# An attention block on one core: the second shifted line of a chain by a transfer in place, without fills on GpSimd

## The chip, the cores and the metric

The kernel runs on one core of a Trainium2 chip. The core's engines are TensorE (matmuls; PE in the profile, its weight loads PEld), VectorE (DVE), ScalarE (ACT), GpSimd (POOL) and SyncE (SP), which only issues transfers here. The metric is the device time of one execution in microseconds, the median of several runs.

## The reference

`x` is 1 x 2048 x 448, `wqkv` 448 x 1344, `wo` 448 x 448, all in bfloat16; 16 heads of 28 channels.

```python
qkv = (x @ wqkv).reshape(B, S, 3, H, Dh).transpose(2, 0, 3, 1, 4)
q, k, v = qkv[0], qkv[1], qkv[2]
scores = einsum("bhqd,bhkd->bhqk", q, k) * Dh ** -0.5
p = softmax(scores, axis=-1)
o = einsum("bhqk,bhkd->bhqd", p, v)
return o.transpose(0, 2, 1, 3).reshape(B, S, D) @ wo
```

## The kernel before

**Tiles and sets.** The 16 heads are four groups (G) of four heads, each head padded to 32 partitions (HP). The 2048 queries are four chunks (c) of 512. A *set* is one group and one chunk, 16 sets in all, worked through in the list `ORDER`. In a set there are 4 heads x 16 blocks of 128 keys = 64 *halves*: one half is the 128 x 512 scores of one head, one block of keys and one chunk of queries. TensorE computes a half from K and Q (`emit_s`, line 780) into PSUM, one of two engines turns it into exponentials in bfloat16 in SBUF, and TensorE multiplies these with V and adds them into the set's output bank `o` (`do_pv`, line 1123). Four such products, one per head, run side by side in the array; they are called a wave. The row of ones that stands beside V in each head's 32 columns makes the softmax's sum come out with the output.

**Two ways to the exponential.** ScalarE takes two halves at once, from a pair of banks `a0` or `a1`, with its exponential function (`do_exp`, line 978), into one of 10 tiles `pt`. VectorE takes single halves from banks `d0`, `d1` and now and then `m`, without an exponential function: it adds a bias, clamps at zero and writes int16 (`do_a`, line 993, tile I). The integer, read as a bfloat16, is 2 to the power of the score with a straight line between powers of two. To smooth this, three such *lines* are summed: I itself, I + 43 and I + 85, as integers, each read as bfloat16 and multiplied with its own copy of V (`WT` = 1, 201/256, 159/256; the scaled copies are made on VectorE, `vs_job`, line 616). So a half on VectorE costs TensorE three products with V, and one on ScalarE a single one.

**Chains.** Four halves of VectorE, one for each head, stand side by side in one I tile of 128 x 2048: a chain. When it is full, the two additions are made for all four at once: line 1 into a tile J1, line 2 into a tile J2 (`do_add`, line 1064; `adds` is the queue of additions due, its third entry the next line to make). Some chains are *far*: when the chain opens with at least `FAR` = 30 halves of its set left, in sets 1 to 14, GpSimd fills the J1 tile with the constant 43 (`far_chain`, line 1029), and when I is full a transfer issued by GpSimd adds I into J1 (`accumulate`, line 1040, `accum_op=ALU.add`). VectorE then makes only line 2. There are 4 I tiles (`NCH`), 4 of J1 (`NJ`) and 3 of J2 (`NCH2`). A chain's tiles are free again when the products with V have used them.

**What sets the order.** The order of all engines' instructions is written out at build time by a planner (`plan`), which plays the program through with fixed costs: 0.904 us for an exponential of ScalarE, 0.6 for an eviction or a full addition on VectorE, 0.226 for a wave, 1.05 for a fill and 0.88 for the issue of an adding transfer on GpSimd, 5.6 from the end of the issue to its landing (`ACC_LAND`). It plays 24 random seeds and keeps the shortest. At each step the engine that is free first picks its next work (`pick_pe`, `pick_act`, `pick_dve`, `pick_pool`, `pick_sp`). VectorE gets a new half whenever a bank `d` is free, so the split between the two engines falls out of how fast VectorE empties its banks. Operations marked `port` on GpSimd and VectorE's additions are never placed at the same time (`port[...]`), and on the chip GpSimd's operations wait for the last such operation of VectorE that the planner placed ahead of them (`after_shared`). Chains open ahead of their set: when fewer than 20 halves of a set are left, VectorE's next chain is of the next set. The products with V, however, go set by set: the bank `o` opens for the next set only when every product of the last one has been made (`finish_set`).

**Other work on the same engines.** The projections of K, Q and V for the later groups run between (`k_job`, `q_job`, `v_job`); GpSimd squares K and Q for a bound on the scores (`square`, line 357) and multiplies finished outputs with the reciprocal of the sums (`mul`, line 1173); GpSimd also clears the tiles of V in the prologue (`clear_v`, line 241). V lies in one tile for each group (groups 2 and 3 together) and block of 512 keys, and so does each of the two scaled copies.

The lines that decide on a far chain:

```python
if sum(len(q) for q in remain[step[0]]) >= (FAR if step[0] < NSET - 1 else LASTFAR) and step[0] >= FIRST:
    ch["far"] = True
    far_chain(ch)
```

Of the kernel before, what the change touches and what calls it, by code (L numbers as in the profile page):

```python
# [9 lines left out]
ALU = mybir.AluOpType  # L10
# [43 lines left out]
def kernel(  # L54
# [36 lines left out]
    NPT = 10  # L91
    NCH = 4
    NCH2 = 3
    NJ = 4
    FAR = 30
    FIRST = 1
# [38 lines left out]
    WO = big.tile([P, G, D], BF16, name="WO")  # L135
    VT = [None] * NTERM
    for k in range(NTERM):
        VT[k] = {}
        for b in range(NXB):
            for g in range(GH):  # L140
                VT[k][g, b] = big.tile([P, XB, P], BF16, name=f"V{k}_{g}_{b}")[:]
        for b in range(NXB):
            t = big.tile([P, XB, G - GH, P], BF16, name=f"V{k}_{GH}_{b}")
            for g in range(GH, G):
                VT[k][g, b] = t[:, :, g - GH, :]
            VT[k][None, b] = t[:]
    xs = [big.tile([P, XB * D if b < NPL else (G - 1) * QW], BF16, name=f"xs{b}") for b in range(NXB)]
# [90 lines left out]
    def clear_v(g, b):  # L238
        v = VT[0][g, b]
        v = v.rearrange("p t g e -> p (t g e)") if g is None else v.rearrange("p t e -> p (t e)")  # L240
        nc.gpsimd.memset(v, 0.0)
        nc.gpsimd.memset(v.rearrange("p (r e) -> p r e", e=HP)[:, :, Dh:Dh + 1], 1.0)

    for g in list(range(GH)) + [None]:
# [13 lines left out]
    def plan(nc, tc, psum, big, wk, dram, seed, dry):  # L258
# [262 lines left out]
        def qn_first(bank, pri):  # L521
            def mm():
                held["qn0"] = (bank_tile(bank) if bank[0] != "a" else pair_tile(bank))[:, 0:QW]
                nc.tensor.matmul(out=held["qn0"], lhsT=maskK[:, 0, :], rhs=sqt.pop(("Q", 0, 0))[:], start=True, stop=True)

            def root():
                held["nq"] = VT[1][None, 0].rearrange("p t g e -> p (t g e)").bitcast(F32)
# [50 lines left out]
        def v_job(g, b, t0, bank, pri, gate=0, eng="DVE"):  # L578
# [7 lines left out]
            def mm(part):  # L586
                if part == 0:
                    held[key] = bank_tile(bank)
                for u in range(part * n // parts, (part + 1) * n // parts):
                    for cc in range(CC):  # L590
                        quarters(held[key][:, u * w:(u + 1) * w], xt(b, cc)[:, (t0 + u) * P:(t0 + u + 1) * P],
                                 WRAW[2][:, cc, g0 * HG * Dh:g1 * HG * Dh], cc == 0, cc == CC - 1)

            def evac():
                src = held.pop(key)[:, 0:n * w].rearrange("p (r e) -> p r e", e=Dh)
                if g is None:
                    dst = VT[0][None, b][:, t0:t0 + n, :, :].rearrange("p t g (i e) -> p (t g i) e", e=HP)
                else:
                    dst = VT[0][g, b].rearrange("p t (i e) -> p (t i) e", e=HP)
                if eng == "ACT":  # L600
                    nc.scalar.copy(out=dst[:, :, 0:Dh], in_=src)
                else:
                    nc.vector.tensor_copy(out=dst[:, :, 0:Dh], in_=src)

# [7 lines left out]

        def vs_job(g, b, pri):
            def scale(k):
                flat = (lambda v: v.rearrange("p t g e -> p (t g e)")) if g is None else (lambda v: v.rearrange("p t e -> p (t e)"))
                cur["shared"] = nc.vector.tensor_scalar(out=flat(VT[k][g, b]), in0=flat(VT[0][g, b]), scalar1=WT[k], scalar2=None, op0=ALU.mult)

            gs = [g] if g is not None else list(range(GH, G))
            for k in range(1, NTERM):
                add("DVE", 0.335 if g is None else 0.2, lambda k=k: scale(k), need=[("V", gs[0], XB * b + u) for u in range(XB)],  # L620
                    gives=[("VS", gg, b, k) for gg in gs], pri=pri + 0.1 * k, port=True)

# [110 lines left out]
        for b in range(NXB):  # L733
            v_job(1, b, 0, "m", 50 + b, STEPS + 10 + 12 * b)
            vs_job(1, b, 60 + b)
        a, z = 2 * STEPS, 2 * NQC * STEPS - 30
        for kt in range(0, NKT, 2):
            v_job(None, kt // XB, kt % XB, "m", 150 + kt, a + (z - a) * kt // NKT)
        for b in range(NXB):
            vs_job(None, b, 170 + b)  # L740
        for c in range(CL):
# [8 lines left out]
        pts_used = [0]  # L750
        chain = {"cur": None, "all": []}
        a_fifo = []
# [107 lines left out]
        def d_more(s, t, acting):  # L860
            got, taken = [], []
            for b in d_banks(t):
# [8 lines left out]
                if ch is None:  # L871
# [133 lines left out]
        def close(ch, m):  # L1005
            ch["m"] = m
            ch["at"] = free["DVE"]
            adds.append([ch, m, 2 if ch["far"] else 1])
            if ch["far"]:
                accumulate(ch, m)  # L1010

        def used_up(ch, k):
# [5 lines left out]
        def add_ok(a):  # L1018
            if a[2] == 1:
                return True  # L1020
            n = chain["all"].index(a[0])
            return n < NCH2 or used_up(chain["all"][n - NCH2], 2)

        def far_chain(ch):
# [8 lines left out]
            add("POOL", 1.05, emit, gives=[("fill", n)], pri=20, port=True)  # L1033

        def accumulate(ch, m):
            w = slice(0, m * QW)
# [5 lines left out]
            def landed(end):  # L1042
                at = ch["acc"] = end + ACC_LAND
                for n in range(m):
# [13 lines left out]
        def do_add(t):  # L1058
# [10 lines left out]
            adds[0][2] += 1  # L1069
            if adds[0][2] == NTERM:  # L1070
                adds.pop(0)
# [8 lines left out]
        def pv_cands(t):  # L1080
# [27 lines left out]
        def do_pv(t, ws):  # L1108
# [9 lines left out]
            for w in ws:  # L1118
                for e in w:
                    _, i, j = e["step"]  # L1120
                    key = (s, i)
                    SETMM[key] = SETMM.get(key, 0) + 1
                    nc.tensor.matmul(out=o[HP * i:HP * (i + 1), :], lhsT=VT[e["k"]][g, j // XB][:, j % XB, HP * i:HP * (i + 1)],  # L1123
                                     rhs=e["ap"], start=(SETMM[key] == 1), stop=False, tile_position=(0, HP * i),
                                     skip_group_check=True)
                for e in w:
# [229 lines left out]

        osb_last = [VT[1][0, hf].rearrange("p t e -> p (t e)").bitcast(F32) for hf in range(2)]
        rT = [wk.tile([P, 2, HG], F32, name=f"rT{hf}", bufs=1) for hf in range(2)]
# [79 lines left out]
```

## Time and profile before

| | |
|---|---|
| median of 3 runs | 360.37 us (360.24 to 360.82) |
| profiled execution | 360.86 us, span 359.1 us |
| TensorE, VectorE, ScalarE busy | 336.9, 333.8, 339.1 us |
| GpSimd busy | 174.3 us |
| exponentials of ScalarE | 358, each of two halves |
| evictions of VectorE | 308, that is 77 chains |
| additions of VectorE | 99 |
| fills and adding transfers of GpSimd | 55 and 55 |

The span is what the profiler sees from the first to the last instruction; the profiled execution's own time is the device time of that same run. A busy time is the union of an engine's instructions. The mean of one ScalarE exponential, 1121 ns, is from its start to its end; consecutive ones overlap, so 358 of them take 330.5 us. In a group's line, the part behind the bar is busy time and mean of one, and then the idle time of the engine before such instructions and what ended most of it. "POOL J L1040 <- DVE I L993" in the waits reads: GpSimd, ahead of its instruction of line 1040 that writes J, was idle until VectorE's instruction of line 993 that writes I. A transfer's time to landing counts from its issue.

### The profile page before, as it was taken

How to read it: one execution, taken by the hardware profiler on the slowest of the kernel's cores; microseconds unless marked ns; L12 is line 12 of the kernel's file. 1: busy time of each engine (PE TensorE's matmuls, PEld its weight loads, DVE VectorE, ACT ScalarE, POOL GpSimd, SP SyncE). 2: the span in 40 equal slices, each digit the busy share in tenths (PEclk: the TensorE clock that was granted, in tenths of full speed). 3: DMA queues.
4: the chain of work that ended last, by engine and by line, in shares of the span. 5: the costliest groups of instructions: out<-in, count | busy, mean ns of one | idle time of the engine just before them, and what ended most of it. 6: DMA issues, size and time to landing. Idle time of an engine off the chain costs nothing.

```text
span 359.1 us, 11135 instructions
## 1 busy us (share of the span) xinstructions
PE 336.9 (94%) x4453; PEld 108.3 (30%) x4454; DVE 333.8 (93%) x615; ACT 339.1 (94%) x370; POOL 174.3 (49%) x215
## 2 busy tenths in 40 slices
PE   8999999999999999999989999998898989999995
PEld 4333233322234233232222222232222222222233
DVE  7889999999999999899999999998999999999973
ACT  3699999999999999999999999999999999999991
POOL 8951563635535474454455656464736464531010
PEclk9999999999999999999999999999999999999999
DMA  9430175664646666364667646565868848674111
GB/s 207 105 96 15 29 150 105 120 135 87 129 89 117 127 120 147 63 136 84 132 127 156 135 90 120 105 136 124 165 120 177 163 89 174 133 156 103 39 48 54
DMA packets 30185, 41.37 MB, mean 115 GB/s; under 512 B 15188, under 2 KB 21172, under 8 KB 30132
## 3 DMA queue, kind: packets, MB, share of 16 engines
q0 software_dynamic: 8368, 28.87, 41.6%
q1 hardware_dynamic: 20516, 11.22, 12.2%
q8 instruction: 35, 0.57, 0.6%
q10 hardware_dynamic: 1248, 0.55, 0.6%
q14 instruction: 18, 0.15, 0.1%
HBM read 6.20 MB, written 1.96 MB: 23 GB/s over the span
## 4 chain that ended last, share of the span: by engine, by line
PE 41%; ACT 32%; DVE 11%; issue 8%; DMA 6%; POOL 1%; SPq 0%; DVEq 0%; POOLq 0%; ACTq 0%
ACT pt L978 32%; PE a L780 14%; PE o L1123 11%; PE m L342 5%; DVE I L993 5%; PE m L335 4%; DMA J<-I 4%; DVE J L1064 2%; DMA rr<-scr 2%; PE o L679 1%; DMA scr<-rec 1%; PE d L780 1%; DVE KA L375 1%; DVE kp L451 1%; PE a L335 1%
## 5 line engine op out<-in xcount | busy, mean ns | idle before, releaser
L978 ACT ACTIVATE pt<-a 128x1024 bf16<-128x1024 f32 x358 | 330.5, 1121 | 3.5 <-PE a L780 1.6
L993 DVE TENSOR_SCALAR I<-d 128x512 int16<-128x512 f32 x276 | 180.3, 680 | 10.6 <-PE d L780 8.4
L780 PE MATMUL a<-QP,KA 32*128 32x512 bf16 (+1 forms) x708 | 138.1, 381 | 11.1 <-ACT pt L978 9.8
L1123 PE MATMUL o<-pt,V 128*32 128x512 bf16 x716 | 108.2, 383 | 0.0
L780 PE MATMUL d<-QP,KA 32*128 32x512 bf16 (+1 forms) x273 | 98.5, 383 | 0.2
L780 PEld LDWEIGHTS <-KA 32*128 32x128 bf16 (+1 forms) x1035 | 45.8, 91 | 145.0 <-issue 143.1
L1123 PE MATMUL o<-J,V 128*32 128x512 bf16 x616 | 87.2, 384 | 0.9 <-DVE J L1064 0.4
L1029 POOL MEMSET J<- 128x1024 int32 x55 | 58.4, 1061 | 48.4 <-PE d L780 13.5
L1040 POOL DMA_DIRECT2D J<-I x55 | 52.7, 957 | 58.1 <-DVE I L993 50.2
L1064 DVE TENSOR_SCALAR J<-I 128x2048 int16<-128x2048 int16 x99 | 73.9, 756 | 0.6
L1123 PE MATMUL o<-I,V 128*32 128x512 bf16 x308 | 68.2, 383 | 0.7 <-DVE o_sb L1150 0.6
L1123 PEld LDWEIGHTS <-V 128*32 128x32 bf16 x1640 | 31.3, 94 | 49.5 <-issue 45.3
L1173 POOL TENSOR_TENSOR xs<-o_sb,rr 128x512 bf16<-128x512 f32 x12 | 17.1, 1429 | 29.9 <-DVE J L1064 20.1
L357 POOL TENSOR_TENSOR sq<-QA 128x512 bf16<-128x512 bf16 x15 | 16.8, 1117 | 21.7 <-DVE QA L497 13.1
L993 DVE TENSOR_SCALAR I<-m 128x512 int16<-128x512 f32 x32 | 21.8, 680 | 0.2 <-PE m L780 0.2
L335 PE MATMUL m<-XT,WRAW 128*32 128x512 bf16 x216 | 18.3, 386 | 0.1
L357 POOL TENSOR_TENSOR sq<-KA 128x512 bf16<-128x512 bf16 x12 | 14.3, 1196 | 8.3 <-DVE KA L375 6.7
L342 PE MATMUL m<-WRAW,XT 128*32 128x112 bf16 (+1 forms) x432 | 13.7, 231 | 0.2
L342 PE MATMUL m<-WO,xs 128*32 128x448 bf16 x156 | 12.5, 359 | 0.0
L780 PE MATMUL m<-QP,KA 32*128 32x512 bf16 (+1 forms) x32 | 12.3, 384 | 0.0
L342 PE MATMUL m<-sq,maskK 128*32 128x512 bf16 x108 | 10.8, 389 | 1.4 <-POOL sq L357 1.2
L497 DVE CAST QA<-m 128x512 bf16<-128x512 f32 x15 | 10.2, 683 | 0.6 <-PE m L335 0.3
(126 smaller groups left out, 226.6 us busy)
## 6 DMA issues: line engine op xcount, KB each, us to landing
J<-I POOLq DMA_DIRECT2D x55, 512.0 KB, 4.9
rr<-scr SPq DMA_DIRECT2D x60, 64.0 KB
QP<-QA SPq DMA_DIRECT2D x60, 28.0 KB
out_dram<-osb SPq DMA_DIRECT2D x12, 112.0 KB
WRAW<-in_wqkv_dram SPq DMA_DIRECT2D x3, 336.0 KB
QP<-su SPq DMA_DIRECT2D x32, 2.0 KB
WO<-in_wo_dram SPq DMA_DIRECT2D x16, 24.5 KB
den<-o_sb SPq DMA_DIRECT2D x15, 8.0 KB
```

Source lines behind the costliest of these rows:

```text
L335: nc.tensor.matmul(out=ps[HP * i:HP * (i + 1), :], lhsT=w[:, cc, h * Dh:h * Dh + HP], rhs=xt(c, cc), start=(cc == 0), stop=(cc == CC - 1), ...
L342: nc.tensor.matmul(out=out[r, :], lhsT=lhsT[:, r], rhs=rhs, start=start, stop=stop, tile_position=(0, HP * i), **k)
L357: after_shared(nc.gpsimd.tensor_tensor(out=t[:], in0=src, in1=src, op=ALU.mult))
L497: nc.vector.tensor_copy(out=t[:], in_=held[key][:, 0:QW])
L780: nc.tensor.matmul(out=out_ap, lhsT=KAt[(g, j // XB)][r, (j % XB) * P:(j % XB + 1) * P], rhs=q[r, :], start=(n == 0), stop=(n == len(terms ...
L978: nc.scalar.activation(out=pt[:], in_=ps[:], func=ACT.Exp, scale=LN2 / 128.0)
L993: nc.vector.tensor_scalar(out=dst, in0=pd[:], scalar1=BIAS, scalar2=0.0, op0=ALU.add, op1=ALU.max)
L1029: m = nc.gpsimd.memset(ch[1][:].bitcast(I32), fill)
L1040: after_shared(nc.gpsimd.dma_start(out=ch[1][:, w], in_=ch["I"][:, w], accum_op=ALU.add))
L1064: cur["shared"] = nc.vector.tensor_scalar(out=r[:, w], in0=ch["I"][:, w], scalar1=float(SHIFT[k]), scalar2=None, op0=ALU.add)
L1123: nc.tensor.matmul(out=o[HP * i:HP * (i + 1), :], lhsT=VT[e["k"]][g, j // XB][:, j % XB, HP * i:HP * (i + 1)], rhs=e["ap"], start=(SETMM[k ...
L1173: m = nc.gpsimd.tensor_tensor(out=otile(g, c), in0=st["o_sb"][:], in1=st["rr"][:], op=ALU.mult)
```

## The change

A chain is now *own* instead of far when it opens with at least `FAR2` = 36 halves of its set left, in sets 1 to 14. For an own chain VectorE makes line 1 into J1, and line 2 is made in the I tile itself: when line 1 is made and the four products of line 0 have read I, GpSimd issues a transfer that adds a constant tile (85 everywhere, `shift2`, filled once in the prologue) onto I (`in_place`). The products of line 2 then read I. Such a chain uses no J2. All other chains get both lines from VectorE. With `FAR` = 99 no chain is far: a set has only 64 halves. There are 6 I tiles and 5 of J1. An I tile of an own chain is free only when line 2 is used, too.

The planner learns that such transfers queue behind each other (`landing`, 3 us each), that products of line 0 of own chains go first, and that those of a line by transfer go last until 1.5 us after it is due.

To make room in SBUF, V of groups 1, 2 and 3 lies in larger tiles, and the scaled copies of groups 0 and 2 share tiles, as do those of groups 1 and 3; the copies of groups 1 and 3 are made by one operation of 2048 for each line, those of 0 and 2 by operations of 512. The projection of V writes its PSUM tile group by group, and two small tiles that had borrowed room in V's copies (`qn_first` and the tail's `osb_last`) take `pt` tiles.

```diff
-    NCH = 4
+    NCH = 6
     NCH2 = 3
-    NJ = 4
-    FAR = 30
+    NJ = 5
+    FAR = 99
+    FAR2 = 36
+    ACC_BUSY = 3.0
...
+    shift2 = const.tile([P, HG * QW], I16, name="shift2")
+    nc.gpsimd.memset(shift2[:].bitcast(I32), SHIFT[2] * 65537)
...
         def vs_job(g, b, pri):
+
             def scale(k):
...
+                if b is None:
+                    src = VT[1][:] if g == 1 else VT[2][:, g - GH, :, :]
+                    dst = VS[k, g] = big.tile([P, NKT, P], BF16, name=f"VW{k}", tag=f"VW{k}", bufs=1)
+                else:
+                    src = v_block(g, b)
+                    dst = VS[k, g, b] = big.tile([P, XB, P], BF16, name=f"VS{k}_{b}", tag=f"VS{k}_{b}", bufs=1)
...
             if chain["cur"] is None and len(chain["all"]) >= NCH:
                 old = chain["all"][-NCH]
                 if not j1_free() or not used_up(old, 0) or any(a[0] is old for a in adds) or old["acc"] is None or old["acc"] > t:
+                    return False
+                if old["own"] and not used_up(old, 2):
                     return False
...
-                    if sum(len(q) for q in remain[step[0]]) >= (FAR if step[0] < NSET - 1 else LASTFAR) and step[0] >= FIRST:
+                    rest = sum(len(q) for q in remain[step[0]])
+                    early = FIRST <= step[0] < NSET - 1
+                    ch["own"] = early and rest >= FAR2
+                    if early and FAR <= rest < FAR2:
...
+        def landing(end):
+            chain["dma"] = max(chain["dma"], end + ACC_LAND - 1.0 - ACC_BUSY) + ACC_BUSY
+            return chain["dma"] + 1.0
+
+        def in_place(ch, m):
+
+            n = ch["id"] = chain["all"].index(ch)
+            w = slice(0, m * QW)
+            if used_up(ch, 0):
+                evt[("PV0", n)] = (free["PE"], "PE")
+
+            def emit():
+                after_shared(nc.gpsimd.dma_start(out=ch["I"][:, w], in_=shift2[:, w], accum_op=ALU.add))
+
+            def landed(end):
+                at = landing(end)
+                for q in range(m):
+                    pending.append({"step": ch["steps"][q], "k": 2, "ap": ch["I"][:, q * QW:(q + 1) * QW].bitcast(BF16),
+                                    "ready": at, "pt": None, "ch": ch})
+
+            add("POOL", 0.88, emit, need=[("line1", n), ("PV0", n)], gives=[("own", n)], pri=9, port=True)
+            ops["POOL"][-1].after = landed
...
+            if ch["own"]:
+                evt[("line1", ch["id"])] = (end, "DVE")
+            if adds[0][2] == NTERM - ch["own"]:
                 adds.pop(0)
...
-            out_.sort(key=lambda e: bool(e["ch"] and e["ch"]["far"] and e["k"] == 1 and t < e["ready"] + 1.5))
+            out_.sort(key=lambda e: 0 if not e["ch"] else -1 if e["ch"]["own"] and e["k"] == 0 else
+                      bool((e["ch"]["far"] and e["k"] == 1 or e["ch"]["own"] and e["k"] == 2) and t < e["ready"] + 1.5))
...
+                        if e["k"] == 0 and e["ch"]["own"] and used_up(e["ch"], 0):
+                            evt[("PV0", e["ch"]["id"])] = (end, "PE")
```

More of the change, by code (lines that the diff above doesn't have):

```diff
@@ L135, with v_of, v_block @@
     WO = big.tile([P, G, D], BF16, name="WO")
[L136 to L146, printed above, removed]
+    VT = {(0, b): big.tile([P, XB, P], BF16, name=f"V0_{b}") for b in range(NXB)}
+    VT[1] = big.tile([P, NKT, P], BF16, name="V1")
+    VT[2] = big.tile([P, G - GH, NKT, P], BF16, name="V2")
+    VS = {}
+    def v_of(k, g, j):
+        if k:
+            return VS[k, g, j // XB][:, j % XB, :] if g % 2 == 0 else VS[k, g][:, j, :]
+        return VT[0, j // XB][:, j % XB, :] if g == 0 else VT[1][:, j, :] if g == 1 else VT[2][:, g - GH, j, :]
+    def v_block(g, b):
+        return VT[0, b][:] if g == 0 else VT[1][:, b * XB:(b + 1) * XB, :] if g == 1 else VT[2][:, g - GH, b * XB:(b + 1) * XB, :]
     xs = [big.tile([P, XB * D if b < NPL else (G - 1) * QW], BF16, name=f"xs{b}") for b in range(NXB)]
@@ L614, in scale @@
             def scale(k):
-                flat = (lambda v: v.rearrange("p t g e -> p (t g e)")) if g is None else (lambda v: v.rearrange("p t e -> p (t e)"))
-                cur["shared"] = nc.vector.tensor_scalar(out=flat(VT[k][g, b]), in0=flat(VT[0][g, b]), scalar1=WT[k], scalar2=None, op0=ALU.mult)
-            gs = [g] if g is not None else list(range(GH, G))
+                if b is None:
[4 more added lines that the diff above has]
+                    dst = VS[k, g, b] = big.tile([P, XB, P], BF16, name=f"VS{k}_{b}", tag=f"VS{k}_{b}", bufs=1)
+                cur["shared"] = nc.vector.tensor_scalar(out=dst[:].rearrange("p t e -> p (t e)"), in0=src.rearrange("p t e -> p (t e)"),
+                                                        scalar1=WT[k], scalar2=None, op0=ALU.mult)
+            blocks = range(NKT) if b is None else range(XB * b, XB * (b + 1))
             for k in range(1, NTERM):
-                add("DVE", 0.335 if g is None else 0.2, lambda k=k: scale(k), need=[("V", gs[0], XB * b + u) for u in range(XB)],
-                    gives=[("VS", gg, b, k) for gg in gs], pri=pri + 0.1 * k, port=True)
+                add("DVE", 0.6 if b is None else 0.2, lambda k=k: scale(k),
+                    need=[("V", g, j) for j in blocks] + ([("Oset", ORDER.index((g - 2, CL)))] if g > 1 else []),
+                    gives=[("VS", g, j // XB, k) for j in blocks[::XB]], pri=pri + 0.1 * k, port=True)
         def oproj_job(c, tq, pri):
@@ L739, in plan @@
         for b in range(NXB):
[L740 removed]
+            vs_job(2, b, 170 + b)
+        vs_job(3, None, 180)
         for c in range(CL):
@@ L750, in plan @@
         pts_used = [0]
-        chain = {"cur": None, "all": []}
+        chain = {"cur": None, "all": [], "J2": [], "dma": 0.0}
         a_fifo = []
@@ L1008, in close @@
             adds.append([ch, m, 2 if ch["far"] else 1])
+            if not ch["own"]:
+                chain["J2"].append(ch)
             if ch["far"]:
                 accumulate(ch, m)
+            elif ch["own"]:
+                in_place(ch, m)
         def used_up(ch, k):
@@ L1042, in landed @@
             def landed(end):
-                at = ch["acc"] = end + ACC_LAND
+                at = ch["acc"] = landing(end)
                 for n in range(m):
@@ L1355, in filler @@
                 more.remove(op)
-        osb_last = [VT[1][0, hf].rearrange("p t e -> p (t e)").bitcast(F32) for hf in range(2)]
+        osb_last = [wk.tile([P, 2 * QW], BF16, name="pt", bufs=NPT)[:, 0:QW].bitcast(F32) for hf in range(2)]
         rT = [wk.tile([P, 2, HG], F32, name=f"rT{hf}", bufs=1) for hf in range(2)]
```

33 lines of the change are left out of this document (17 added, 16 removed).

## The prediction

> **What bounds the kernel now.** I read the page's busy times first, then its groups of instructions, then the waits, and then one long window of the steady part, from 20 to 340 us.
>
> ```profile
> PE 336.9 (94%) x4453; PEld 108.3 (30%) x4454; DVE 333.8 (93%) x615; ACT 339.1 (94%) x370; POOL 174.3 (49%) x215
> ...
> PE 41%; ACT 32%; DVE 11%; issue 8%; DMA 6%; POOL 1%; SPq 0%; DVEq 0%; POOLq 0%; ACTq 0%
> ...
> L978 ACT ACTIVATE pt<-a 128x1024 bf16<-128x1024 f32 x358 | 330.5, 1121 | 3.5 <-PE a L780 1.6
> L993 DVE TENSOR_SCALAR I<-d 128x512 int16<-128x512 f32 x276 | 180.3, 680 | 10.6 <-PE d L780 8.4
> ...
> L1123 PE MATMUL o<-J,V 128*32 128x512 bf16 x616 | 87.2, 384 | 0.9 <-DVE J L1064 0.4
> ...
> L1029 POOL MEMSET J<- 128x1024 int32 x55 | 58.4, 1061 | 48.4 <-PE d L780 13.5
> L1040 POOL DMA_DIRECT2D J<-I x55 | 52.7, 957 | 58.1 <-DVE I L993 50.2
> L1064 DVE TENSOR_SCALAR J<-I 128x2048 int16<-128x2048 int16 x99 | 73.9, 756 | 0.6
> ...
> L993 DVE TENSOR_SCALAR I<-m 128x512 int16<-128x512 f32 x32 | 21.8, 680 | 0.2 <-PE m L780 0.2
> ```
>
> Three engines are full at once. The steady window says it more sharply (columns: window, its length, then PE, PEld, DVE, ACT, POOL):
>
> ```profile
> 20.00:340.00 320.00, 304.23 (x3977) 94.28 (x3975) 308.14 (x523) 317.43 (x346) 154.65 (x162) 1.00 0.56 116
> ```
>
> ScalarE misses 2.6 us of 320, VectorE 11.9, TensorE 15.8. GpSimd is half idle, so its fills are not a bound in themselves. The work is one pool of 1024 score blocks ("halves" of 128x512): 358 exponentials take two each (716), and VectorE takes 276 + 32 = 308, in chains of four, which is 77 chains. So the length of the steady part is the number of exponentials times their price, and each chain more on VectorE takes two exponentials, 2 x 330.5/358 = 1.85 us, off ScalarE. What the change does to the time therefore hangs on one question: does VectorE get room for more chains, and do the lines still come in time for TensorE?
>
> ```profile
> PE a L780 <- ACT pt L978: 9.8, 30, 0.5
> DVE I L993 <- PE d L780: 8.4, 25, 1.1
> DVE I L993 <- PE m L780: 1.4, 4, 0.5
> POOL J L1040 <- DVE I L993: 50.2, 31, 4.2
> PEld L1123 <- DMA J<-I: 1.2, 2, 0.8
> PE o L1123 <- DMA J<-I: 0.4, 1, 0.4
> ```
>
> TensorE waits for ScalarE to free a score bank (9.8 us), VectorE for its next scores (9.8 us over two rows), and TensorE for the accumulating transfers only 1.6 us in all: 55 transfers are hidden almost completely now.
>
> **The change, part by part.**
>
> *The 55 fills and the longer prologue.* The fills' 58.4 us leave GpSimd; off the path, worth nothing directly. The prologue gets one fill for the constant tile and sixteen clears of 512 elements in place of eight of 512 and four of 1024.
>
> ```profile
> 8.65 0.55 POOL L241 MEMSET V<- 128x512 bf16 x1
> 9.26 0.17 POOL L242 MEMSET V<- 128x16 bf16 x1
> 9.30 0.97 POOL L241 MEMSET V<- 128x1024 bf16 x1
> ...
> 14.03 7.70 POOL L226 DMA_DIRECT2D QP<-offs  x14
> ...
> 22.15 0.53 POOL L254 TENSOR_SCALAR_AFFINE_SELECT self__165<-self__165 128x4 f32<-128x4 f32 x1
> 27.24 1.04 POOL L357 TENSOR_TENSOR sq<-QA 128x512 bf16<-128x512 bf16 x1 [4.56 <-DVE QA L497]
> ```
>
> A block of 512 takes 0.65 us from start to start (8.65 to 9.30), one of 1024 takes (14.03 - 9.30)/4 = 1.18; 16 x 0.65 - 8 x 0.65 - 4 x 1.18 = +0.5 us, and 1.06 for the constant tile. The 1.6 us is hidden by the 4.56 us in which GpSimd then has nothing to do; without that cover the first square would be late by 1.6.
>
> *VectorE's additions.* Now 99 = 77 x 2 - 55. After it, only chains that open with at least 36 halves of their set left (it was 30) are served by a transfer. A chain opens every 1024/77 = 13.3 halves, so six halves less in 14 sets cost 14 x 6/13.3 = 6.3 chains; counted in the order that the planner wrote for the kernel before, 48 open at 36 or more. I take 48: additions 77 x 2 - 48 = 106, seven more.
>
> ```profile
> 33.19 0.69 DVE L1064 TENSOR_SCALAR J<-I 128x2048 int16<-128x2048 int16 x1
> 33.80 1.28 DVE L993 TENSOR_SCALAR I<-d 128x512 int16<-128x512 f32 x2
> 34.99 0.68 DVE L497 CAST QA<-m 128x512 bf16<-128x512 f32 x1
> ```
>
> An undisturbed addition occupies 0.61 us from its start to the next start (33.19 to 33.80), an eviction (34.99 - 33.80)/2 = 0.60. Seven additions: +4.3 us of VectorE.
>
> *What the fills did to the additions.* Seven of the 99 ran beside a fill, the first and the last of them being
>
> ```profile
> 120.98 1.18 DVE L1064 TENSOR_SCALAR J<-I 128x2048 int16<-128x2048 int16 x1
> ...
> 299.40 0.68 DVE L1064 TENSOR_SCALAR J<-I 128x2048 int16<-128x2048 int16 x1
> ```
>
> ```profile
> L1064 DVE TENSOR_SCALAR J<-I x99: 628/683/1565, 21.9 to 347.1; 128x2048 int16<-128x2048 int16 x99
> ...
> L1040 POOL DMA_DIRECT2D J<-I x55: 851/873/1422, 43.7 to 321.9; - x55
> ...
> DMA to landing us min/median/max: 4.4/4.9/6.6
> ```
>
> The seven lasted 7.9 us together against 7 x 0.683 = 4.8 at the median: 3.1 us are saved. All 99 exceed the median by 99 x (0.756 - 0.683) = 7.2 us, so the saving lies between 0 (other GpSimd work moves into the fills' place) and 7.2; 3.1 is what is seen beside fills.
>
> Here a rule of the Trainium skill bears, page "SBUF — State Buffer", section "SBUF: two separate sides": VectorE in a two-port mode and GpSimd hold a shared port pair exclusively, for a whole instruction. The trace agrees in kind, 0.68 us becoming 1.18 beside a fill; if each of the 55 fills cost an addition the same 0.5 us, the rule would make the saving an estimated 27 us, but the 99 additions lost only 7.2 in all.
>
> *The scaled copies of V.* Sixteen operations of 512 and eight of 1024 become sixteen of 512 and four of 2048, which I price as an addition, of the same 2048 two-byte elements: 4 x 0.683 - 8 x 0.498 = -1.25 us.
>
> ```profile
> L616 DVE TENSOR_SCALAR V<-V 128x512 bf16<-128x512 bf16 x16 | 4.9, 348 | 0.0
> ...
> L616 DVE TENSOR_SCALAR V<-V 128x1024 bf16<-128x1024 bf16 x8 | 3.7, 498 | 0.0
> ```
>
> Sum of VectorE's own work: +4.3 - 3.1 - 1.25 = about 0. At unchanged chains VectorE gains nothing.
>
> *The room in the order.* The planner keeps an addition back while it has a GpSimd operation under way. With 58.4 us of fills and 7 x 0.957 = 6.7 us of issues gone, GpSimd's 154.65 us in the window fall to 89.6, from 48% to 28% of it. If the 9.8 us in which VectorE waited for scores shrink by the same 42%, because an addition can now be put into such a gap, 4.1 us come free (between 0, if the gaps remain for want of scores, and 11.9, all of the idle time). One chain costs VectorE 4 x 0.60 + (106/77) x 0.61 = 3.24 us. So 4.1 us carry one more chain, not two: 78 chains, 356 exponentials, **-1.85 us**. TensorE gets eight more matmuls for it, 8 x 87.2/616 = 1.1 us, under its 15.8.
>
> *The second line by transfer, in place.* Before, the transfer of line 1 went out as soon as the chain was evicted. Now it waits for the J addition (0.68) and for the four I matmuls on TensorE, and then needs 0.957 + 4.9 us. Queued behind it on GpSimd are the squares for the next projections and the multiplies of finished outputs. GpSimd already sat 50.2 us in front of the old transfer, longest 4.2, so I cost the new wait at nothing there.
>
> At a set's end: a chain that opens at 36 halves has 36 x 320/1024 = 11.3 us until its set's last half, and uses 13.3 x 0.3125 = 4.2 to fill, 0.7 to add, 0.4 for the matmuls, 0.96 and 4.9 for the transfer: 11.2. Exactly bare at the threshold, covered by 0.3125 us for every half above it. At a set's start two or three chains stand finished, and their transfers go out together.
>
> ```profile
> q0 software_dynamic: 8368, 28.87, 41.6%
> ```
>
> One transfer occupies the 16 engines for 0.416 x 359.1/55 = 2.7 us, so the third of a bunch lands some 5.4 us after the first, about 12 us into a set of 20: hidden, since TensorE has the I and J lines of the same chains until then. Bounds: -1.6 us (every wait on transfers goes) and +4.2 (each of 14 sets ends 0.3 us late). I take **+0.6**: of these ends the measured one is the nearer, as the transfers' length and number hardly change, and it is on the side of a loss because 3 of the 48 chains opened at 36 to 39 halves, with little to cover them. The greater number of I and J buffers (6 and 5 for 4 and 4) covers the longer life of I; I cost it at nothing, and at up to one chain (1.85 us) if a chain's start had to wait for a transfer.
>
> *Sum.* -1.85 + 0.6 = -1.25 us. The profiled execution took 360.86 us (span 359.1), 0.49 above the median of 360.37; off the median it gives **359.1 us**.
>
> **The rivals.**
>
> 1. *Late second lines (slower).* The last transfer of a set lands after everything else of it, TensorE cannot open the next set, its backlog grows and the score banks of ScalarE starve. For it: the bare 11.2 against 11.3 us at the threshold, and landings up to 6.6. Against: TensorE lost only 1.6 us to transfers so far. It decides from 0.13 us in each of 14 sets (1.85/14), where the gain of the chain is used up; at the bound above, 0.3 us in each, it gives 360.4 + 4.2 - 1.85 = 362.7.
> A sentence of the same section of the Trainium skill speaks for this rival: GpSimd cannot write a transfer's descriptors while VectorE holds the port, so seven more additions mean more late transfers. No wait on a transfer over 0.8 us is in this trace.
> 2. *No more chains (same).* VectorE's gaps come from scores that are not there, not from GpSimd: 77 chains, 0 + 0.6 and less 0.5 for the squares that come sooner (they cost two longer waits now): 360.4.
> 3. *Two or three chains more.* All of the 11.9 us goes to chains: 11.9/3.24 = 3.6, held at two by TensorE's and VectorE's own lateness: 360.4 - 3.7 + 0.6 = 357.3.
> 4. *A chain fewer.* The seven additions fall where VectorE is fullest, at the set ends, and 4.3 us is more than one chain: 360.4 + 1.85 = 362.2.
>
> That the change does not do what it says is excluded for the fills: the code that emits them is reached no more.
>
> **How the numbers follow.** Forecast 0.32, late lines 0.18, no more chains 0.22, two or more 0.14, a chain fewer 0.14. About 0.2% (0.7 us) is what the measurement can tell. Faster by more: 0.27 of the forecast, 0.14 of the third rival, 0.07 of the second: 0.48. Within: 0.04 + 0.10 = 0.14. Slower: the first and fourth and 0.05 of the second, and a little of the forecast: 0.38. Range 356.7 to 363.6: below, rival 3 less 0.6; above, rival 1 and half a chain (0.9) more. The forecast's own range is 358.0 to 360.0.
>
> **What would show it.** The line of fills is gone and one of 128x1024 stands in the prologue. Additions number 104 to 110, 0.70 to 0.73 us each on average. Exponentials: 356 shows the gained chain, 358 rival 2, 354 or fewer rival 3, 360 rival 4. GpSimd's busy time falls to 105 to 115 us. In the waits, TensorE for transfers at 1 to 3 us supports the sum; 4 or more, with ScalarE's idle time up from 3.5, is rival 1. The prediction is wrong if the exponentials are as forecast and the time is not lower, since then stalls ate the chain.

## The result, and the profile after

The changed kernel takes 359.26 us in the median of 20 executions (358.49 to 360.37), the kernel before 360.68 beside it (20 executions, 359.97 to 361.93): a ratio of 0.9959, interval 0.9949 to 0.9969. It is faster by 1.4 us, where 1.25 were forecast. The profile says at once that it is not faster for the reason given. From the page after (busy times, then the groups):

```profile
PE 338.0 (94%) x4474; PEld 110.3 (31%) x4474; DVE 329.4 (92%) x616; ACT 338.1 (94%) x370; POOL 115.3 (32%) x164
...
L1001 ACT ACTIVATE pt<-a 128x1024 bf16<-128x1024 f32 x358 | 329.5, 1167 | 3.2 <-PE d L798 1.7
L1016 DVE TENSOR_SCALAR I<-d 128x512 int16<-128x512 f32 x278 | 181.4, 680 | 9.2 <-PE d L798 8.6
...
L1074 POOL DMA_DIRECT2D I<-shift x50 | 44.0, 941 | 99.9 <-PE o L1176 28.4
L1114 DVE TENSOR_SCALAR J<-I 128x2048 int16<-128x2048 int16 x104 | 72.9, 709 | 0.7
```

There are 358 exponentials, as before, and 278 + 30 evictions, as before: 77 chains, not 78. The fills are gone, 50 transfers took the place of 55, and there are 104 additions. The steady window (same columns as in the prediction), the by-form groups of the scaled copies of V, two waits and the landing of the transfers:

```profile
20.00:340.00 320.00, 306.37 (x4025) 96.90 (x4021) 308.27 (x532) 317.75 (x347) 95.89 (x104) 1.00 0.53 109
```

```profile
L631 DVE TENSOR_SCALAR VS<-V 128x512 bf16<-128x512 bf16 x16 | 3.9, 284 | 0.0
...
L631 DVE TENSOR_SCALAR VW<-V 128x2048 bf16<-128x2048 bf16 x4 | 2.6, 683 | 0.0
```

```profile
DVE I L1016 <- PE d L798: 8.6, 25, 1.1
...
PE o L1176 <- DMA I<-shift: 0.4, 1, 0.4
```

```profile
DMA to landing us min/median/max: 4.5/6.0/9.7
```

GpSimd's 154.65 us in the window have become 95.89, for the 89.6 worked out; VectorE's idle time in it is 11.7 us, where it was 11.9, so none of that became room. What did change is how steadily ScalarE runs. A ScalarE line's busy time plus the idle time before it is the whole stretch of the exponentials: 330.5 + 3.5 = 334.0 us before, 329.5 + 3.2 = 332.7 after. At 358 exponentials in both, and with 0.904 us from one start to the next in the median of both traces, the 1.3 us are waits of ScalarE that went away. These are single executions: the profiled one of the changed kernel took 360.29 us, 1.0 above its median, that of the kernel before 360.86, 0.2 above, so the pair is only 0.6 us apart and need not show what the medians do. I use this sum for every kernel below, and ratios to the kernel before, which was measured beside each on the same chip.

### The profile page after: what moved, and what is told of

Read it like the earlier page. It is cut to its first block, busy times and chain, and to the rows that moved or that the text cites. A ratio compares the mean times of both kernels' runs of the same rounds, so it can differ in the third digit from the quotient of the medians.

```text
span 358.2 us, 11057 instructions
## 1 busy us (share of the span) xinstructions
PE 338.0 (94%) x4474; PEld 110.3 (31%) x4474; DVE 329.4 (92%) x616; ACT 338.1 (94%) x370; POOL 115.3 (32%) x164
## 4 chain that ended last, share of the span: by engine, by line
PE 45%; ACT 37%; issue 7%; DVE 6%; DMA 3%; POOL 0%; SPq 0%; POOLq 0%; ACTq 0%; DVEq 0%
ACT pt L1001 37%; PE a L798 17%; PE o L1176 13%; PE m L341 5%; PE m L348 5%; DVE I L1016 3%; DMA scr<-rec 2%; PE o L696 1%; DVE J L1114 1%; DVE kp L457 1%; DMA rr<-scr 1%; PE d L348 1%; PE d L798 1%; PE a L341 1%; DVE V L612 0%
## 5 line engine op out<-in xcount | busy, mean ns | idle before, releaser
L1001 ACT ACTIVATE pt<-a 128x1024 bf16<-128x1024 f32 x358 | 329.5, 1167 | 3.2 <-PE d L798 1.7
L1176 PE MATMUL o<-pt,V 128*32 128x512 bf16 x716 | 102.7, 383 | 0.0
L798 PE MATMUL d<-QP,KA 32*128 32x512 bf16 x275 | 95.4, 384 | 0.8 <-DVE I L1016 0.8
L1074 POOL DMA_DIRECT2D I<-shift x50 | 44.0, 941 | 99.9 <-PE o L1176 28.4
L1176 PE MATMUL o<-I,V 128*32 128x512 bf16 x308 | 60.0, 385 | 0.0
L1176 PE MATMUL o<-J,VS 128*32 128x512 bf16 x212 | 36.0, 383 | 0.0
L1176 PEld LDWEIGHTS <-V 128*32 128x32 bf16 x1024 | 26.8, 94 | 29.8 <-issue 29.1
L1176 PE MATMUL o<-J,VW 128*32 128x512 bf16 x204 | 31.3, 384 | 0.0
L1228 POOL TENSOR_TENSOR OTL<-o_sb,rr 128x512 bf16<-128x512 f32 x3 | 3.8, 1264 | 34.4 <-DMA rr<-scr 21.7
L1176 PE MATMUL o<-I,VW 128*32 128x512 bf16 x108 | 13.7, 385 | 0.0
L1176 PEld LDWEIGHTS <-VS 128*32 128x32 bf16 x304 | 10.1, 94 | 9.3 <-issue 8.7
```

The source lines that it names most:

```text
L798: nc.tensor.matmul(out=out_ap, lhsT=KAt[(g, j // XB)][r, (j % XB) * P:(j % XB + 1) * P], rhs=q[r, :], start=(n == 0), stop=(n == len(terms ...
L1001: nc.scalar.activation(out=pt[:], in_=ps[:], func=ACT.Exp, scale=LN2 / 128.0)
L1074: after_shared(nc.gpsimd.dma_start(out=ch["I"][:, w], in_=shift2[:, w], accum_op=ALU.add))
L1176: nc.tensor.matmul(out=o[HP * i:HP * (i + 1), :], lhsT=v_of(e["k"], g, j)[:, HP * i:HP * (i + 1)], rhs=e["ap"], start=(SETMM[key] == 1), s ...
L1228: m = nc.gpsimd.tensor_tensor(out=otile(g, c), in0=st["o_sb"][:], in1=st["rr"][:], op=ALU.mult)
```

## The experiments

| kernel | ratio to before, interval | median us | exponentials | their stretch, us |
|---|---|---|---|---|
| changed | 0.9959 (0.9949 to 0.9969) | 359.26 | 358 | 332.7 |
| e1 copy for the accumulation, fills kept | 0.9911 (0.9889 to 0.9933) | 357.84 | 358 | 330.6 |
| e2 the same without fills | 0.9895 (0.9873 to 0.9917) | 357.26 | 358 | 330.0 |
| e3 changed, with useless fills | 1.0055 (1.0036 to 1.0075) | 363.05 | 358 | 335.6 |
| e4 changed, constant tile filled early | 0.9943 (0.9923 to 0.9963) | 359.08 | 358 | 332.3 |
| e5 changed, copy for the accumulation | 0.9911 (0.9899 to 0.9924) | 357.99 | 358 | 331.2 |
| e6 new layout of V alone | 0.9918 (0.9905 to 0.9930) | 358.29 | 358 | 332.6 |
| e7 e4 with FAR2 = 30 | 0.9963 (0.9948 to 0.9977) | 360.17 | 356 | 332.8 |
| e8 e4 with FAR2 = 24 | 0.9970 (0.9955 to 0.9985) | 359.93 | 354 | 330.0 |
| e9 before, other order | 0.9944 (0.9931 to 0.9957) | 358.51 | 358 | 331.7 |
| e10 before, third order | 0.9975 (0.9965 to 0.9985) | 359.67 | 358 | 332.3 |
| e11 new layout and buffers, old chains | 0.9929 (0.9910 to 0.9949) | 358.01 | 358 | 330.4 |
| e12 changed, other order | 0.9956 (0.9938 to 0.9974) | 359.78 | 358 | 333.2 |

The rows e1 to e12 have 4 to 12 executions each. The stretch is from one profiled execution each and need not be a typical one: for e6 and e8 that execution took 360.07 and 358.81 us (medians 358.29 and 359.93), for the changed kernel 360.29.

**e1 and e2: do the fills cost anything where they stood?** The fills cannot simply be left out of the kernel before, since an accumulation needs a tile to add to; that was not tried. So both copy I into J1, and e2 issues no fill.

```diff
-                after_shared(nc.gpsimd.dma_start(out=ch[1][:, w], in_=ch["I"][:, w], accum_op=ALU.add))
+                after_shared(nc.gpsimd.dma_start(out=ch[1][:, w], in_=ch["I"][:, w]))
...
-                m = nc.gpsimd.memset(ch[1][:].bitcast(I32), fill)
-                after_shared(m)
+                pass
```

The first pair of lines is e1; e2 has both.

> The kernel before, with its transfers copying I into J1 instead of adding it (line 1 then lacks its 43, so the output is not the reference's), the fills kept: every engine's order is that of the kernel before. It is the partner of e2_copy_nofill. Both theories expect the time of the kernel before, 360.7, or up to 0.5 less, since a copy may land earlier than an accumulation and the transfers hold TensorE up by only 1.6 us.

> The same with the 55 fills not issued, and the order of VectorE, TensorE, ScalarE and SyncE unchanged. Theory (fills collide with additions, and ScalarE starves behind them): 1.0 to 2.0 us less than e1_copy_fill, about 359.2, with an addition's mean falling from about 756 to about 710 ns. Rival (the new order is what is faster, the fills cost nothing): the same time as e1_copy_fill within 0.4 us.

ScalarE's line and the additions' on e1's page, GpSimd's transfers in e1 by the tile they write (duration in ns: least, median, most; then their landing), and ScalarE's line on e2's page:

```profile
L978 ACT ACTIVATE pt<-a 128x1024 bf16<-128x1024 f32 x358 | 329.2, 1162 | 1.4 <-PE a L780 0.8
...
L1064 DVE TENSOR_SCALAR J<-I 128x2048 int16<-128x2048 int16 x99 | 69.0, 707 | 0.6
```

```profile
L1040 POOL DMA_DIRECT2D J<-I x55: 527/591/965, 43.3 to 318.1; - x55
...
DMA to landing us min/median/max: 2.8/3.0/5.3
```

```profile
L978 ACT ACTIVATE pt<-a 128x1024 bf16<-128x1024 f32 x358 | 328.9, 1172 | 1.1 <-PE a L780 0.7
```

Both theories failed on e1: the swap alone took 0.9% (3.2 us) off, where at most 0.5 was expected. A transfer that accumulates is issued in 0.873 us and lands after 4.9 in the median, one that copies in 0.591 and 3.0, and this was worth as much as any other step in the study, although TensorE's waits named transfers for 1.6 us only. The additions show one way: their mean fell from 756 to 707 ns with every fill still there. The chain of work that ended last in the kernel before shows another: two of the 55 transfers lie on it (start and length in us), and on e1's chain there is none.

```profile
178.82 6.50 DMA J<-I
...
237.26 6.60 DMA J<-I
```

How the 3.2 us divide between issue, landing and additions is not shown. The fills themselves, e2 against e1, cost 0.6 us (medians 357.84 and 357.26; the executions, 357.73 to 358.29 and 357.19 to 357.73, hardly overlap), less than the 1.0 to 2.0 that the theory expected and more than the rival's 0.4, and with the quicker transfers around them.

**e3: the fills put back.** Each own chain issues a useless fill of its J1 tile; the planner does not see it.

```diff
-                    if early and FAR <= rest < FAR2:
-                        ch["far"] = True
+                    if ch["own"]:
                         far_chain(ch)
...
-            add("POOL", 1.05, emit, gives=[("fill", n)], pri=20, port=True)
+            add("POOL", 0.0, emit, gives=[("fill", n)], pri=20)
```

> The changed kernel with one useless fill of J1 for each own chain put back on GpSimd, which the planner does not see, so that the order on the other four engines is that of the changed kernel. Theory (collisions): 1.0 to 2.5 us above the changed kernel's 359.3, additions over 730 ns in the mean. Rival (order): 359.3 within 0.4 us.

```profile
L1001 ACT ACTIVATE pt<-a 128x1024 bf16<-128x1024 f32 x358 | 330.6, 1123 | 5.0 <-PE m L798 1.6
...
L1114 DVE TENSOR_SCALAR J<-I 128x2048 int16<-128x2048 int16 x104 | 77.2, 751 | 1.2
```

1% (3.5 us by the ratios) over the changed kernel, at the same order on the other four engines, and more than the 2.5 expected. The additions grew by 4.3 us in all and ScalarE's stretch by 2.9. So fills that fall where no room was planned for them do cost, and collisions with additions are at least part of the price. In these two cases some 50 fills cost 0.6 us (e2: planned for, with quick transfers) and 3.5 (e3: not planned for).

**e4: the constant tile's fill.** The timelines of VectorE, GpSimd and ScalarE in the profiled execution of the changed kernel (start and length in us):

```profile
22.30 1.91 DVE L1114 TENSOR_SCALAR J<-I 128x2048 int16<-128x2048 int16 x1
```

```profile
22.68 0.97 POOL L257 MEMSET shift<- 128x1024 int32 x1
```

```profile
26.13 4.73 ACT L1001 ACTIVATE pt<-a 128x1024 bf16<-128x1024 f32 x5 [0.89 <-PE d L798]
```

The one fill left meets an addition, which takes 1.91 us for 0.68, and ScalarE stands for 0.89.

```diff
+    shift2 = const.tile([P, HG * QW], I16, name="shift2")
+    nc.gpsimd.memset(shift2[:].bitcast(I32), SHIFT[2] * 65537)
     for g in range(G):
         for b in range(NXB):
             clear_v(g, b)
...
-    shift2 = const.tile([P, HG * QW], I16, name="shift2")
-    nc.gpsimd.memset(shift2[:].bitcast(I32), SHIFT[2] * 65537)
```

> The changed kernel with the one fill of the constant tile moved ahead of the clears of V in GpSimd's prologue; nothing else moves. In the profiled execution of the changed kernel that fill ran beside the second addition, which took 1.9 us, and ScalarE's next exponential came 1.0 us late. Theory: this is so in most executions, and the time falls by 0.5 to 1.0 us to about 358.5. Rival: the late transfers of offsets behind it cost as much, or the collision is of that one execution: 359.3 within 0.3 us.

The same place in e4, VectorE and ScalarE:

```profile
22.26 0.69 DVE L1114 TENSOR_SCALAR J<-I 128x2048 int16<-128x2048 int16 x1
```

```profile
19.36 11.34 ACT L1001 ACTIVATE pt<-a 128x1024 bf16<-128x1024 f32 x12 [0.19 <-PE d L798]
```

The collision and the gap are gone. The ratio is 0.9943 for 0.9959, 0.6 us, but the intervals overlap and the medians are only 0.2 us apart, so a gain over all executions is not shown. More speaks for the rival, that the collision belongs to single executions. The fill stands in the same place in e3, e5, e6, e11 and e12. In the profiled executions of e3, e5, e11 and e12 the addition at this place took 0.69 us and ScalarE's gap was 0.19 at most; the next addition, where the fill or the GpSimd operations behind it met that one, took 0.68 to 1.05. In e5:

```profile
21.68 0.69 DVE L1114 TENSOR_SCALAR J<-I 128x2048 int16<-128x2048 int16 x1
...
24.02 1.05 DVE L1114 TENSOR_SCALAR J<-I 128x2048 int16<-128x2048 int16 x1
```

Only e6 shows a larger gap, 0.43 us, and its profiled execution, like the changed kernel's, was a long one, 1.8 us above the median.

**e5: do the transfers in place still cost?**

```diff
-                after_shared(nc.gpsimd.dma_start(out=ch["I"][:, w], in_=shift2[:, w], accum_op=ALU.add))
+                after_shared(nc.gpsimd.dma_start(out=ch["I"][:, w], in_=shift2[:, w]))
```

> The changed kernel with the transfer copying the constant tile over I instead of adding it (line 2 is then no line of the scores, so the output is not the reference's); every order is that of the changed kernel. In the kernel before, the same swap (e1_copy_fill) took 3.4 us off: a copy is issued in 0.59 us for 0.87 and lands after 3.0 us for 4.9. Theory (in the changed kernel the transfers are hidden at the sets' ends and keep no addition waiting): at most 0.7 us less than the changed kernel, 358.6 or more. Rival (the transfers' issue or landing still sets part of the time): 1.5 to 3 us less, about 357.

```profile
L1001 ACT ACTIVATE pt<-a 128x1024 bf16<-128x1024 f32 x358 | 329.3, 1179 | 1.9 <-PE a L798 0.8
...
L1114 DVE TENSOR_SCALAR J<-I 128x2048 int16<-128x2048 int16 x104 | 70.9, 690 | 0.7
```

1.7 us less than the changed kernel by the ratios, inside what the rival expected. So the accumulations still cost the changed kernel something, but half of the 3.2 us that they cost the kernel before.

**e6 and e11: the layout without the new chains.** Both run the changed code with chains, fills and transfers as before; e6 with the old numbers of tiles, e11 with the new ones.

```diff
-    NCH = 6
+    NCH = 4
...
-    NJ = 5
-    FAR = 99
-    FAR2 = 36
+    NJ = 4
+    FAR = 30
+    FAR2 = 99
```

e11 has the last two lines of it only.

> The changed kernel's code with FAR = 30, FAR2 = 99, 4 tiles of I and 4 of J1: chains, fills and transfers as in the kernel before, with the new layout of V and its scaled copies alone (and one fill of a constant tile that nothing reads). Theory (the layout is no part of the gain): 360 to 362, the kernel before plus what its order differs by, 0.8 us by the planner's own account. Rival (fewer and larger scaled copies, 2.2 us less of VectorE, are the gain): 359.5 or less.

> The changed kernel with FAR = 30 and FAR2 = 99 and its 6 and 5 tiles of I and J1: layout and buffers of the changed kernel, chains, fills and transfers of the kernel before (77 chains; 345.7 us by the planner's account). Theory (layout): 358.0 to 358.8, as e6_layout, whose order is another. Rival (draws): anywhere from 358 to 361.5; and if the second line in place is itself a gain, 359.3 or more.

e11's page:

```profile
L1001 ACT ACTIVATE pt<-a 128x1024 bf16<-128x1024 f32 x358 | 329.1, 1141 | 1.3 <-PE a L798 1.1
...
L1056 POOL MEMSET J<- 128x1024 int32 x56 | 59.3, 1072 | 46.9 <-PE d L798 18.6
```

Here the time forecast for e6 by the theory that the layout is no part of the gain (360 to 362) was missed, and the rival's (359.5 or less) came: with 56 fills each, these two are at 0.9918 and 0.9929 the fastest of the study but for the copying ones. They beat the kernel before by 2.6 to 3 us, and the changed one by 1.1 (e11) and 1.5 (e6), e6's interval lying wholly below the changed kernel's. Between e11 and the changed kernel the code differs only in which early chains get a line by transfer (from 30 halves or from 36) and in how that line is made, and the old way with its fills came out faster, the intervals just touching. But a different chain makes a different order, and that had to be weighed by itself.

**e9, e10 and e12: the same work in another order.** The planner keeps the shortest of 24 orders; these keep another one.

```diff
-    seed = min(ends, key=lambda k: ends[k])
+    seed = 18
```

(9 in e10, 11 in e12.)

> The kernel before with the planner's second best order (seed 18 for 14; 77 chains in both, 345.8 us for 345.6 by the planner's own account): not a line of work differs. Theory (the new layout of V is the gain, 2.2 us less of VectorE): 360.4 to 361.8, as the kernel before. Rival (what an order loses on the chip beyond the planner's account differs from draw to draw by as much as the change): more than 0.8 us from the kernel before's 361.1, on either side.

> The kernel before with its third best order (seed 9; 77 chains, 346.1 us by the planner's account). Theory (layout): 360.7 to 362.1. Rival (draws): more than 0.8 us away from the kernel before, and not by the planner's 0.5.

> The changed kernel with its second best order (seed 11 for 5; 77 chains in both, 345.5 us for 345.4 by the planner's account). Theory (draws): as the kernel before moved by 2.1 and 1.0 us between draws, this one lies 0.5 us or more from 359.3, on either side. Rival (an order without fills loses less at random, since GpSimd's work is what an order's loss depends on): within 0.4 us of 359.3.

ScalarE's line in e9, in e10 and in e12:

```profile
L978 ACT ACTIVATE pt<-a 128x1024 bf16<-128x1024 f32 x358 | 329.7, 1134 | 2.0 <-PE a L780 1.2
```

```profile
L978 ACT ACTIVATE pt<-a 128x1024 bf16<-128x1024 f32 x358 | 329.9, 1135 | 2.4 <-PE a L780 1.6
```

```profile
L1001 ACT ACTIVATE pt<-a 128x1024 bf16<-128x1024 f32 x358 | 329.4, 1150 | 3.8 <-PE d L798 2.0
```

The kernel before, with not a line of its code changed, is 2.0 us faster in the planner's second best order and 0.9 in its third best (which has one far chain more); its own pick is the slowest of the three on the chip, although the planner rates them within 0.5 us. So e9 and e10 bear out the rival, that orders differ by as much as the change. e12 does not: the second order of the changed kernel has the ratio of its first (0.9956), with a wider spread. That is what its rival had said, where the theory wanted 0.5 us or more of difference. So for the kernel before the draw of an order is worth as much as the change: the changed kernel's 0.9959 and 0.9956 lie between the other two draws of the kernel before, 0.9944 and 0.9975.

The additions of e10 and of e12:

```profile
L1064 DVE TENSOR_SCALAR J<-I 128x2048 int16<-128x2048 int16 x98 | 73.3, 765 | 0.4
```

```profile
L1114 DVE TENSOR_SCALAR J<-I 128x2048 int16<-128x2048 int16 x105 | 71.3, 688 | 0.6
```

e10 is faster than the kernel before although its additions are slower (765 ns for 756), and e12, with the shortest additions of all the kernels, is no faster than the changed one. So what the additions lose to GpSimd does not by itself decide the time of an order.

**e7 and e8: more chains.** e4 with a lower threshold; the planner then finds room for 78 and 79 chains.

```diff
-    FAR2 = 36
+    FAR2 = 30
```

(24 in e8.)

> e4_fill_early with FAR2 = 30: chains that open with 30 to 35 halves left are served by transfers, too. The planner then makes 78 chains and 356 exponentials instead of 77 and 358, with 54 transfers. Theory (a chain more is worth two exponentials, 1.85 us, and the cover at the sets' ends still holds): 357.3. Rival (chains that open so late land after their set's other lines, and TensorE waits): 359.1 or more, with TensorE's waits for transfers over 2 us.

> The same with FAR2 = 24: 79 chains, 354 exponentials and 61 transfers in the planner's order. Theory: two chains more than e4_fill_early, 3.7 us less, less some waits: 355.5 to 357. Rival (late lines): 359 or more, waits of TensorE for transfers over 3 us.

The pages have 356 and 354 exponentials; the times did not follow. ScalarE's line in e7 and in e8:

```profile
L1001 ACT ACTIVATE pt<-a 128x1024 bf16<-128x1024 f32 x356 | 328.5, 1134 | 4.3 <-PE a L798 2.9
```

```profile
L1001 ACT ACTIVATE pt<-a 128x1024 bf16<-128x1024 f32 x354 | 326.0, 1155 | 4.0 <-PE o L1176 2.7
```

Busy time falls by 1.1 us in e7 and 3.6 in e8 against e4's 329.6, and idle time takes 1.6 and 1.3 back. By the ratios e7 is 0.7 and e8 1.0 us behind e4; the intervals overlap, so it is not shown that they are slower, but the gains of 1.85 and 3.7 us did not come. Neither lost them as the rival said: no wait of TensorE for one of these transfers stands in either trace, and its longest single wait in e7 names GpSimd's squares (1.5 us, below). In e8 ScalarE waits 2.7 us for products with V, that is, for free `pt` tiles: TensorE is behind. And e8's order leaves one block of the output projection until after the last exponentials, which none of the other kernels does:

```profile
352.82 0.53 ACT L1456 CAST osb<-a 128x448 bf16<-128x448 f32 x1 [1.87 <-DMA out_dram<-pt]
```

Its ends take 26.7 us outside the stretch, e4's 25.5, so 1.2 us more were lost there.

## Why the prediction was right, and where it was not

Its time (359.1) and its sign were right; its main term was not. The chain that was to bring 1.85 us did not come, and waits that the sum held at nothing went away instead. That the two came out alike is luck.

*What bounds the kernel*: right. In every kernel of the table the stretch of ScalarE's exponentials is all of the span but some 25 us (e8: 27) at the two ends.

*The room in the order*: this is the step that failed. It let VectorE's waits for scores shrink by 42%, as GpSimd's share of the window did, and made a 78th chain of it. GpSimd's share fell nearly as worked out, from 154.65 to 95.89 us (89.6 forecast); the waits for scores went from 9.8 us to 8.6 and VectorE's idle time from 11.9 to 11.7. By the planner's own account (its dry run, from 20 to 335 us of its time) VectorE's idle time with an addition kept back by GpSimd fell from 17.4 to 5.4 us, while its idle time for want of scores rose from 4.3 to 10.0. That is the lower bound the prediction had named (the gaps remain for want of scores) and the mechanism of its second rival; by the prediction's own signs 358 exponentials meant that rival, whose time, 360.4 and so no change, did not come either. The term measured 0 exponentials for -1.85 us. The planner's dry run has 77 chains in both kernels, and 345.4 us after for 345.6 before, so it could have told this without the chip. Nor did further chains bring 1.85 us each in e7 and e8, where waits took back part of what ScalarE saved in busy time; these are one order each, so what a chain is worth in general is not shown.

*The additions*: 104 for 106, since 50 chains and not 48 open at 36 or more. Their excess over the median was 7.2 us before and is 104 x (0.709 - 0.682) = 2.8 after, so 4.4 were saved for 3.1 predicted, within the bounds. What of the 7.2 did not lie beside fills lay, in the trace before, beside GpSimd's squares and multiplies (4.2 us).

*The copies of V*: 8.6 us have become 6.5, -2.1 for -1.25; the operations of 2048 take 683 ns as priced, and those of 512 fell from 348 to 284. Little of that need be the layout: in e9, which has the old one, the copies take 6.8 us, and in e6 and e11, which have the new one, 7.2 and 7.0.

*The prologue*: costed at nothing, hidden by 4.56 us in which GpSimd had nothing to do. The cover was counted on GpSimd, and there it held; in the profiled execution a loss arose on VectorE instead, whose addition met the fill (22.30 us, 1.91 long), and it cost ScalarE 0.89 us. It did not arise in four of the six profiled executions with the fill in that place (e3, e5, e11, e12).

*The second line in place*: TensorE's own waits for transfers fell to 0.4 us, below the 1 to 3 expected, although a transfer now lands after 6.0 us for 4.9: the cover at the sets' ends held. The sum's +0.6 was not seen as such. But "hidden" was too simple a word: e5 shows 1.7 us that hang on the accumulations by ways that no wait of TensorE names.

*The sum*: in place of 1.85 us for a chain, ScalarE's waits shrank, by 1.3 us in the profiled pair. That collisions of fills and additions are part of this is supported by e3 and e2 and by the additions' own means; that they are all of it is not shown, and e10 and e12 speak against it. Two things remain open. One is how much of the 1.4 us belongs to the change at all: the kernel before gains 2.0 and 0.9 us by other draws of its order, so a comparison of single orders cannot tell. The other is why the layout with the old chains (e6, e11) is the fastest: the copies of V save only 1.4 and 1.6 us there against the kernel before and none against e9, and its two orders may be good draws.

## What to carry to other kernels

When an order is written out by a planner, compare several of its orders of each kernel before believing a difference of half a per cent: here the same work spread over 2 us. Before forecasting more room from less work, run the planner and count what it made of it. Work taken off a half-idle engine is worth only what the bounding engine waited because of it; look for that in collisions and late starts, not in busy time, and ask what the freed engine would have to do next. When a fixed cost moves into the prologue, look at what the other engines do at that moment, not only at the idle time of the one that executes it, and look at more than one execution before believing a collision.

## What the runs showed of the hardware

*An accumulating transfer is dear.* 512 KB from SBUF to SBUF, issued by GpSimd, took 0.873 us to issue and 4.9 to land when it added, 0.591 and 3.0 when it copied (e1), and 0.870 and 6.0 against 0.530 and 3.2 in place (e5). Swapping it took 3.2 and 1.7 us off kernels whose TensorE waited for it 1.6 and 0.4 us.

*After a single wait TensorE can run at half its clock for a while.* e7 by 2 us windows (the share of the clock granted is the third column from the right; busy times of PE, PEld, DVE, ACT, POOL ahead of it), and the wait that came first:

```profile
84.00:86.00 2.00, 0.79 (x11) 0.24 (x4) 1.94 (x3) 2.00 (x3) 2.00 (x2) 1.00 0.17 43
86.00:88.00 2.00, 1.71 (x13) 0.33 (x12) 0.80 (x2) 0.45 (x2) 1.24 (x2) 0.65 0.11 29
88.00:90.00 2.00, 2.00 (x17) 0.40 (x14) 1.97 (x4) 1.66 (x2) 0.59 (x1) 0.50 0.15 33
90.00:92.00 2.00, 2.00 (x28) 0.56 (x30) 1.71 (x4) 1.79 (x2) 0.28 (x1) 1.00 0.67 131
```

```profile
PE m L348 <- POOL sq L363: 1.5, 1, 1.5
```

GpSimd's squares came late, TensorE stood for 1.5 us, and then ran at half its clock until 90 us, by the two windows for (0.35/0.5 + 1) x 2 = 3.4 us. e12 has one such dip, after a wait of 1.6 us; in e3 the longest wait of TensorE in the steady part was 1.1 us, and its clock stayed at 1.00. Executions of e12 whose mean clock is 0.995 or less took 360.16 us in the mean (6 of them), the others 358.93; in e7 ten of eleven were such, 359.99 in the mean, and the one other took 358.27. So part of what e7 lost is probably this, and a chain more may be worth something in an order without such a wait; that was not tried. The Trainium skill, page "TensorE: Matmul & The Clock Gate", section "What's actually happening", has the clock fall to half after at least one idle window of about 3.4 us, and rise again after at least one busy window of about that length. The length of the dip, 3.4 us, agrees with the second; the wait ahead of it was 1.5 us, so here less than a whole idle window sufficed.
